# Attention with cached keys: another order of the keys, V loaded in longer runs, and the softmax denominator as two partial sums

## The chip, the cores and the metric

The kernel runs on one core of one Trainium2 chip. The metric is the time of one execution on the device in microseconds. A core has five engines with queues of their own: TensorE (PE in the profile, its weight loads PEld), VectorE (DVE), ScalarE (ACT), GpSimd (POOL) and SyncE (SP, which issues DMAs here). SBUF is the on-chip memory of 128 partitions, PSUM the memory that matmuls write into.

## The reference

Two blocks with an adaptive layer norm: attention with cached keys and values, then a mixer with an MLP. The change is in the first. Cut to it:

```python
def _A_ref(x, k_cache, v_cache, wq, wo):           # x: 2048 x 640, caches: 32 heads x 2048 keys x 128
    q = (x @ wq) ...                               # 32 heads x 2048 queries x 128
    scores = jnp.einsum('bhqd,bhkd->bhqk', q, k_cache) * Dh ** (-0.5)
    p = _softmax(scores, axis=-1)
    o = jnp.einsum('bhqk,bhkd->bhqd', p, v_cache)
    return (...o...).reshape(B, Sq, H * Dh) @ wo
...
h = _layernorm(x) * (1 + ca) + sa
x = x + ga * _A_ref(h, A_k_cache, A_v_cache, A_wq, A_wo)
h = _layernorm(x) * (1 + cb) + sb
x = x + gb * _B_ref(h, B_w1, B_w2, B_w3, B_w4)
```

All tensors are bf16. The softmax sums over all 2048 keys of a head, so the order in which the keys are taken does not matter as long as K and V follow the same order.

## The kernel before

**Stages.** A short start (layer norm, modulation, the first head's queries), the attention loop, the output projection with the second layer norm, and the mixer and MLP. The change lies in the loop and in what is set up for it.

**The loop.** 32 heads of 16 query tiles of 128 rows: 512 steps, and some more to drain. The program is written out by hand, step by step (line 516), as operations that each name what they read and write; a small planner (`Prog`, line 12) turns that into semaphore waits. Each engine runs its operations in the order in which they are written. A step s with tile j of head h has:

- `qk` (L286): 4 matmuls of 128x512 into Sps, two for each half of the 2048 keys.
- VectorE L559, once per half: reads the scores from PSUM, writes them negated and scaled into negS (three buffers) and accumulates the minimum per row. Its second row in the profile is DVE_READ_ACCUMULATOR.
- GpSimd L569: the smaller of the two minima, the bias of the exp.
- ScalarE L572: the exp over 2048 keys, into one of 8 slots of Pb.
- the transpose of that tile of probabilities, so that keys lie on partitions: by a DMA transpose from SyncE's queue (`transpose`, L222, one or two tiles at a time), for tiles 3 and 10 of each head by TensorE (`t_piece` L253, and copies L262 on ScalarE or L264 on VectorE). The target is one of 12 slots of PTs.
- `pv` (L299), 8 to 11 steps later: 16 matmuls of a tile, one for each 128 keys, with the transposed probabilities as weights and V as the moving operand. V lies in SBUF as `Vaug`, 16 groups of 130 columns: 128 of V, then two columns of ones. A matmul reads 129 of them, so column 128 of the result is the sum of the probabilities. Two tiles share a PSUM bank, 130 columns apart.
- ScalarE L550: copies two tiles' results from PSUM into Of.
- GpSimd, four steps after `pv`: for each four tiles `rcp` (L440, 128x4, the power -1 of the sums), then `norm` for each tile (L447, 128x128), and after the fourth a DMA that stores them to o_scratch in HBM (L454, issued on GpSimd).
- one fifth of the next head's query projection (`q_piece` L237, copied by `q_evac` L244) in most half steps.

**Loads of the next head.** All go out on SyncE's queue, in order with the transposes: K in tile 2 (`load_k`, L205, a DMA transpose from HBM, key k into column k), wq in tile 6 (L209), V in tile 12 (`load_v`, L214). K, V and wq have two buffers each. V's DMA takes key 128 t + p to partition p, group t: runs of 256 B.

**On GpSimd's queue.** In a step the L569 of that step comes first, then `rcp` and `norm`. An operation of GpSimd that reads what the operation before it wrote waits on a semaphore for it.

`small` is a small tensor for statistics of the first layer norm (columns 0 to 63, not needed in the loop, where columns 0 to 3 hold -1 for `rcp`) and for the minima and the reciprocals.

Of the kernel before, what the change touches and what calls it, by code (L numbers as in the profile page):

```python
# [7 lines left out]
BF16 = mybir.dt.bfloat16  # L8
F32 = mybir.dt.float32
# [106 lines left out]
def bass_adaLN_cond__mha_block_cached__mixer_s_mlp__prompt_kernel(  # L116
# [6 lines left out]
    KT = D // 128  # L123
    NQT = SQ // 128
    NQC = SQ // 512
    NKT = SK // 128
# [11 lines left out]
    with ExitStack() as es:  # L138
# [11 lines left out]
        if True:  # L150
            with ExitStack() as es1:
# [9 lines left out]
                kv = sb1("kv", [128, 2 * SK + 2 * NKT * 130 + 2 * KT * 128 + 2 * SQ], BF16)  # L161
                small = sb1("small", [128, 4 * NQT + 32], F32)
                hTx = sb1("hTx", [128, US], BF16)
# [4 lines left out]
                rstd = small[:, 3 * NQT:4 * NQT]  # L168
                nm0, nm1, nm, rl = [small[:, 4 * NQT + 8 * i:4 * NQT + 8 * i + 8] for i in range(4)]
                hT = hTx[:, 0:KT * SQ].rearrange("p (k q) -> p k q", k=KT)  # L170
# [3 lines left out]
                KTs = kv[:, 0:o1].rearrange("p (b s) -> p b s", b=2)  # L174
                Vaug = kv[:, o1:o2].rearrange("p (b k d) -> p b k d", b=2, k=NKT)
                wq = kv[:, o2:o3].rearrange("p (b k d) -> p b k d", b=2, k=KT)
# [26 lines left out]
                def load_k(h):  # L203
                    hb = h % 2
                    G.dma("sync", lambda e: e.dma_start_transpose(KTs[:, hb], A_k_cache[0, h]), ("k", hb), w=[("KT", hb)])  # L205

# [5 lines left out]
                def load_v(h):  # L212
                    hb = h % 2
                    G.dma("sync", lambda e: e.dma_start(Vaug[:, hb, :, 0:128], A_v_cache[0, h].rearrange("(t p) d -> p t d", p=128)),  # L214
                          ("v", hb), w=[("V", hb)])
# [76 lines left out]
                def pv(g, half):  # L292
                    hb = (g // NQT) % 2
                    b = g % RPT
                    ob = PO[:, ((g // 2) % 2) * 512 + (g % 2) * 130:]

                    def f(t):
                        for kt in range(half * 8, half * 8 + 8):
                            ins = t.matmul(ob[:, 0:129], PTs[:, b, kt, :], Vaug[:, hb, kt, 0:129],  # L299
                                           start=(kt == 0), stop=(kt == NKT - 1))  # L300
                        return ins
                    G.op("tensor", f, r=[("PT", b, half), ("V", hb), "ones"], w=[("O", (g // 2) % 2)])

# [28 lines left out]
                if H > 1:  # L332
# [8 lines left out]
                     r=["id0"], w=["ident"])  # L341
                G.op("gpsimd", lambda g: g.memset(Vaug[:, :, :, 128:130], 1.0), w=["ones"])
                G.op("scalar", lambda a: a.activation(s_col, c_sb, ACT.Silu), r=["c"], w=["scol"])
# [78 lines left out]
                mone = small[:, 0:4]  # L422
                G.op("gpsimd", lambda g: g.memset(mone, -1.0), w=["mone"] + [("mv", t) for t in range(NQT)])
                bank(("q", 0, NQC - 1))
# [13 lines left out]
                def rcp(gr):  # L438
                    b = gr % 2
                    G.op("gpsimd", lambda g: g.tensor_tensor(  # L440
                        out=rl[:, 4 * b:4 * b + 4], in0=Of[:].rearrange("p a z d -> p (a z) d")[:, 4 * b:4 * b + 4, 128],
                        in1=mone, op=ALU.pow),
                         r=[("Of", 2 * b), ("Of", 2 * b + 1), "mone"], w=[("rl", b)])

                def norm(gr, z):
                    b = gr % 2
                    G.op("gpsimd", lambda g: g.tensor_scalar(  # L447
                        out=On[:, b, z, :], in0=Of[:, 2 * b + z // 2, z % 2, 0:128],
                        scalar1=rl[:, 4 * b + z:4 * b + z + 1], scalar2=1.0, op0=ALU.mult, op1=ALU.mult),
                        r=[("Of", 2 * b + z // 2), ("rl", b)], w=[("On", b, z)])  # L450
# [65 lines left out]
                for s in range(at[-1] + LAG + 1):  # L516
                    h, j = divmod(s, NQT)
                    pvs = PVS.get(s, [])
                    evacs = []
                    if s <= 2:  # L520
                        for i in ((0,), (1, 2), range(3, len(MROW)))[s]:
                            mod_rows(i)
# [26 lines left out]
                    for p in [g_ // 2 for g_ in pvs if g_ % 2 == 1]:  # L549
                        G.op("scalar", lambda a, p=p: a.copy(  # L550
                            Of[:, p % 4].rearrange("p z d -> p (z d)")[:, 0:259], PO[:, (p % 2) * 512:(p % 2) * 512 + 259]),
                            r=[("O", p % 2)], w=[("Of", p % 4)])
# [291 lines left out]
```

## Time and profile before

| | |
|---|---|
| time, median of 3 runs | 1614.81 us (1610.35 to 1619.43) |
| the profiled execution, its time | 1604.1 us |
| its span, from first to last instruction | 1602.3 us |
| mean granted TensorE clock | 0.993 |
| busy share of the span: PE, DVE, ACT, POOL | 93%, 87%, 80%, 39% |
| DMA, mean over the span | 208 GB/s, 1,167,730 packets, 1,148,304 of them under 512 B |
| V load | 32 x 512 KB, 5.2 us from issue to landing (median) |
| K load, a transpose | 32, 4.6 us |
| transposes of probabilities | 256, 7.1 us |
| store of results to o_scratch | 128 x 128 KB, 4.5 us |

The profile is of one execution. Its groups name an operation as line, engine, operation, output<-input, shape and count, then its busy time in us and the mean of one in ns, then the idle time of the engine before it and what ended it. Overlapping rows of an engine count once in its busy time, and a single matmul's duration includes its latency, so the distance between starts is the better measure of its cost. The chain of waits follows back, from the last instruction of a window, what released each step. The issue of a DMA transpose on SyncE's queue has a duration that includes waiting for room.

### The profile page before, as it was taken

What the parts mean: (1) busy time and instruction counts of PE and PEld (TensorE: products, weight loads), DVE (VectorE), ACT (ScalarE), POOL (GpSimd) and SP (SyncE); (2) the same over time, 40 slices, a digit from 0 to 9 for tenths busy, and PEclk for the clock granted to TensorE, in tenths of its full rate; (3) what the DMA queues carried; (4) which work ended last, traced back from release to release, by engine and by line L of the source; (5) the groups of instructions that cost most, each with busy time, mean ns of one, the idle gap of its engine ahead of it and who ended that gap; (6) DMA issues with size and microseconds to landing.
All of it is one profiled execution on the core that took longest, in us unless ns stands there. A gap on an engine that the chain in (4) does not pass through costs nothing.

```text
span 1602.3 us, 34804 instructions
## 1 busy us (share of the span) xinstructions
PE 1492.6 (93%) x13978; PEld 963.0 (60%) x14231; DVE 1392.5 (87%) x2460; ACT 1288.2 (80%) x1145; POOL 622.8 (39%) x1394
## 2 busy tenths in 40 slices
PE   5799999999999999999999999999999799999998
PEld 3466666666666666666666666666666555545444
DVE  6999999999999999999999999999999266666424
ACT  4999999999999999999999999999999300055330
POOL 0144444444444444444444444444444423322000
PEclk9999999999999999999999999999999899999999
DMA  9999999999999999999999999999999994530000
GB/s 305 229 230 239 238 243 237 253 241 240 237 237 233 239 237 237 239 239 247 243 250 246 250 239 235 246 228 239 236 244 244 241 196 106 106 111 1 17 17 34
DMA packets 1167730, 333.62 MB, mean 208 GB/s; under 512 B 1148304, under 2 KB 1161552, under 8 KB 1167568
## 3 DMA queue, kind: packets, MB, share of 16 engines
q1 hardware_dynamic: 1161424, 314.59, 98.3%
q0 software_dynamic: 6144, 16.79, 3.3%
q8 instruction: 112, 1.84, 0.5%
q14 instruction: 50, 0.41, 0.1%
HBM read 43.48 MB, written 19.40 MB: 39 GB/s over the span
## 4 chain that ended last, share of the span: by engine, by line
DVE 30%; ACT 24%; PE 20%; DMA 15%; issue 10%; POOL 0%; SPq 0%; ACTq 0%; DVEq 0%
DVE negS L559 27%; ACT ring L572 19%; DMA ring<-ring 13%; PE Sps L631 8%; PE Sps L772 4%; PE Oaug L756 2%; PE QPp L756 2%; ACT ring L262 2%; ACT Of L550 2%; PE Sps L741 1%; ACT kv L244 1%; DMA ring<-in_A_x_dram 1%; DVE ring L364 1%; DMA negS<-o_scratch 1%; PE Sps L286 1%
## 5 line engine op out<-in xcount | busy, mean ns | idle before, releaser
L559 DVE TENSOR_SCALAR_CACHE_REDUCE negS<-Sps 128x1024 f32<-128x1024 f32 x1024 | 1177.2, 1220 | 22.2 <-PE Sps L286 12.5
L572 ACT ACTIVATE ring<-negS,small 128x2048 bf16<-128x2048 f32 x512 | 1011.4, 2029 | 21.9 <-DMA ring<-ring 15.7
L299 PEld LDWEIGHTS PTp<-kv,ring 128*128 128x128 bf16 x8192 | 560.0, 98 | 245.0 <-DMA ring<-ring 6.7
L286 PE MATMUL Sps<-kv 128*128 128x512 bf16 x1949 | 596.3, 383 | 62.8 <-DVE negS L559 42.9
L299 PE MATMUL PTp<-kv,ring 128*128 128x129 bf16 x8192 | 645.6, 221 | 6.5 <-DMA ring<-ring 5.6
L569 POOL TENSOR_SCALAR small<-small 128x1 f32<-128x1 f32 x512 | 145.8, 285 | 621.5 <-DVE negS L559 621.4
L286 PEld LDWEIGHTS Sps<-kv 128*128 128x128 bf16 x2048 | 124.5, 97 | 187.2 <-DVE negS L559 158.0
L447 POOL TENSOR_SCALAR On<-Of,small 128x128 bf16<-128x128 f32 x512 | 189.8, 371 | 13.0
L669 ACT COPY kv<-PTp 128x640 bf16<-128x640 bf16 x32 | 22.0, 692 | 155.0 <-PE PTp L666 154.9
L440 POOL TENSOR_TENSOR small<-Of,small 128x4 f32<-128x4 f32 x128 | 133.2, 1040 | 6.3 <-ACT Of L550 6.2
L454 POOL DMA_DIRECT2D o_scratch<-On x128 | 103.1, 806 | 40.8 <-POOL On L447 37.2
L237 PE MATMUL Oaug<-hTx,kv 128*128 128x512 bf16 x265 | 101.2, 387 | 7.9 <-ACT ring L262 4.2
L550 ACT COPY Of<-PTp 128x259 f32<-128x259 f32 x256 | 99.5, 389 | 10.5 <-PE PTp L299 10.5
L237 PE MATMUL QPp<-hTx,kv 128*128 128x512 bf16 x259 | 97.5, 381 | 2.5 <-ACT hTx L391 1.8
L559 DVE DVE_READ_ACCUMULATOR negS<-Sps 128x1 f32 x1024 | 85.4, 83 | 0.0
L612 POOL TENSOR_SCALAR On<-On 128x1 f32<-128x1 f32 x48 | 24.3, 507 | 152.9 <-DVE On L621 152.9
L639 DVE TENSOR_TENSOR ring<-Sps,mod_bc 128x640 f32<-128x640 f32 x16 | 13.2, 825 | 77.0 <-PE Sps L631 77.0
L631 PE MATMUL Sps<-wo,hTx 128*128 128x128 bf16 (+1 forms) x504 | 71.8, 304 | 5.0 <-DMA hTx<-o_scratch 4.7
L776 DVE TENSOR_TENSOR ring<-Sps,ring 128x640 f32<-128x640 f32 x16 | 13.2, 825 | 66.2 <-PE Sps L772 66.2
L631 PE MATMUL Sps<-wo,negS 128*128 128x128 bf16 (+1 forms) x504 | 69.1, 298 | 1.3 <-DMA negS<-o_scratch 0.9
L262 ACT COPY ring<-Oaug 128x1024 bf16<-128x1024 bf16 x64 | 66.2, 1034 | 0.0
L631 PEld LDWEIGHTS Sps<-wo,hTx 128*128 128x128 bf16 x512 | 40.2, 99 | 36.9 <-DMA hTx<-o_scratch 4.5
(82 smaller groups left out, 1011.2 us busy)
## 6 DMA issues: line engine op xcount, KB each, us to landing
kv<-in_A_v_cache_dram SPq DMA_DIRECT2D x32, 512.0 KB, 5.2
o_scratch<-On POOLq DMA_DIRECT2D x128, 128.0 KB, 4.5
ring<-in_A_x_dram SPq DMA_DIRECT2D x8, 640.0 KB, 4.9
kv<-in_A_wq_dram SPq DMA_DIRECT2D x32, 160.0 KB, 3.6
wo<-in_A_wo_dram SPq DMA_DIRECT2D x1, 5120.0 KB, 16.4
ring<-ring SPq DMA_TRANSPOSE x256, 7.1
ring<-in_w_mod_dram SPq DMA_DIRECT2D x1, 3200.0 KB, 13.6
out_dram<-wo SPq DMA_DIRECT2D x16, 160.0 KB, 1.8
```

The lines of the kernel that those rows point to most:

```text
L237: G.op("tensor", lambda t: t.matmul(JB[jb], wq[:, hb, q, :], hT[:, q, cc * 512:(cc + 1) * 512], start=(q == 0), stop=(q == KT - 1)), r=[(" ...
L262: G.op("scalar", lambda a: a.copy(dst, src), r=[("J", jb)], w=[("PT", g % RPT, r)])
L286: ins = t.matmul(Sps[:, col:col + 512], QT[:, hb, j * 128:(j + 1) * 128], KTs[:, hb, col:col + 512], start=True, stop=True)
L299: ins = t.matmul(ob[:, 0:129], PTs[:, b, kt, :], Vaug[:, hb, kt, 0:129], start=(kt == 0), stop=(kt == NKT - 1))
L440: G.op("gpsimd", lambda g: g.tensor_tensor(out=rl[:, 4 * b:4 * b + 4], in0=Of[:].rearrange("p a z d -> p (a z) d")[:, 4 * b:4 * b + 4, 128 ...
L447: G.op("gpsimd", lambda g: g.tensor_scalar(out=On[:, b, z, :], in0=Of[:, 2 * b + z // 2, z % 2, 0:128], scalar1=rl[:, 4 * b + z:4 * b + z ...
L454: G.dma("gpsimd", lambda e: e.dma_start(o_scr[jj // 2:jj // 2 + 2, :, hh].rearrange("a p z d -> p a (z d)"), On[:, b].rearrange("p (a z) d ...
L550: G.op("scalar", lambda a, p=p: a.copy(Of[:, p % 4].rearrange("p z d -> p (z d)")[:, 0:259], PO[:, (p % 2) * 512:(p % 2) * 512 + 259]), r= ...
L559: G.op("vector", lambda v, half=half, s=s, r8=r8: v.tensor_scalar(out=negS[:, s % 3, half * 1024:(half + 1) * 1024], in0=Sps[:, half * 102 ...
L569: G.op("gpsimd", lambda g, r8=r8: g.tensor_scalar(out=nm[:, r8:r8 + 1], in0=nm0[:, r8:r8 + 1], scalar1=nm1[:, r8:r8 + 1], scalar2=None, op ...
L572: G.op("scalar", lambda a, s=s, r8=r8: a.activation(Pb[:, s % RPB, :], negS[:, s % 3, :], ACT.Exp, bias=nm[:, r8:r8 + 1], scale=-1.0), r=[ ...
L631: ins = t.matmul(YB[b][:, c0:c0 + cw], OTj[pr % 2][:, 2 * hh + z, :], wo[:, hh, c0:c0 + cw], start=(hh == 0), stop=(hh == H - 1))
```

## The change

**Order of the keys.** Key 16 p + c now lies on partition p, in group c. K is loaded by a DMA transpose whose source is seen as 128 rows of 2048 elements (4096 B, 16 keys), in 16 blocks of 128 columns. The scores' columns, the probabilities and their transposes follow the same order.

**V.** A partition's 16 keys are consecutive in HBM (4096 B). The DMA writes them as 8 runs of two keys (512 B). In SBUF such a run lies between two columns of ones on either side (260 columns for two keys, the same room as before). The matmul of an even group reads the ones column ahead of its key and the key; that of an odd group reads the key and the ones column behind it. The first writes columns 0 to 128 of the result, the second columns 1 to 129: the values fall on columns 1 to 128 in both, the sum over even groups on column 0, that over odd groups on column 129.

**The first group.** The matmul that starts a tile has to set all 130 columns. So the first group reads from `V0`, which holds a one, the first key's values and a zero. Its two edge columns are set once; GpSimd copies the values from Vaug once a head, in tile 2, ahead of that step's L569. V0 lies in `small`, where the layer norm's statistics were.

**The sum.** ScalarE copies 260 columns of a pair of tiles instead of 259. GpSimd adds the two partial sums (128x4) and then takes the power -1.

```diff
-                small = sb1("small", [128, 4 * NQT + 32], F32)
+                small = sb1("small", [128, 4 + 130 + 2 + 32], F32)
...
+                V0 = small[:, 4:134].bitcast(BF16).rearrange("p (b d) -> p b d", b=2)
...
-                Vaug = kv[:, o1:o2].rearrange("p (b k d) -> p b k d", b=2, k=NKT)
+                Vaug = kv[:, o1:o2].rearrange("p (b k d) -> p b k d", b=2, k=NKT // 2)
...
-                    G.dma("sync", lambda e: e.dma_start_transpose(KTs[:, hb], A_k_cache[0, h]), ("k", hb), w=[("KT", hb)])
+                    G.dma("sync", lambda e: e.dma_start_transpose(
+                        KTs[:, hb].rearrange("p (c q) -> p c q", c=NKT), A_k_cache[0, h].rearrange("(q c) d -> q (c d)", c=NKT)), ("k", hb), w=[("KT", hb)])
...
-                    G.dma("sync", lambda e: e.dma_start(Vaug[:, hb, :, 0:128], A_v_cache[0, h].rearrange("(t p) d -> p t d", p=128)),
+                    G.dma("sync", lambda e: e.dma_start(Vaug[:, hb, :, 2:258], A_v_cache[0, h].rearrange("(p t z) d -> p t (z d)", t=NKT // 2, z=2)),
                           ("v", hb), w=[("V", hb)])
...
                         for kt in range(half * 8, half * 8 + 8):
-                            ins = t.matmul(ob[:, 0:129], PTs[:, b, kt, :], Vaug[:, hb, kt, 0:129],
+                            ins = t.matmul(ob[:, 0:130] if kt == 0 else ob[:, kt % 2:kt % 2 + 129], PTs[:, b, kt, :],
+                                           V0[:, hb] if kt == 0 else Vaug[:, hb, kt // 2, (1, 130)[kt % 2]:(130, 259)[kt % 2]],
                                            start=(kt == 0), stop=(kt == NKT - 1))
...
-                G.op("gpsimd", lambda g: g.memset(Vaug[:, :, :, 128:130], 1.0), w=["ones"])
+                for c0 in (0, 258):
+                    G.op("gpsimd", lambda g, c0=c0: g.memset(Vaug[:, :, :, c0:c0 + 2], 1.0), w=[("ones", c0)])
...
+                G.op("gpsimd", lambda g: g.memset(V0[:, :, 0:1], 1.0), w=["v0o"] + SMK)
+                G.op("gpsimd", lambda g: g.memset(V0[:, :, 129:130], 0.0), r=["v0o"], w=["v0e"])
...
                     G.op("gpsimd", lambda g: g.tensor_tensor(
-                        out=rl[:, 4 * b:4 * b + 4], in0=Of[:].rearrange("p a z d -> p (a z) d")[:, 4 * b:4 * b + 4, 128],
-                        in1=mone, op=ALU.pow),
+                        out=rl[:, 4 * b:4 * b + 4], in0=Og[:, :, 0], in1=Og[:, :, 129], op=ALU.add),
+                         r=[("Of", 2 * b), ("Of", 2 * b + 1)], w=[("rs", b), ("rl", b)])
+                    G.op("gpsimd", lambda g: g.tensor_tensor(
+                        out=rl[:, 4 * b:4 * b + 4], in0=rl[:, 4 * b:4 * b + 4], in1=mone, op=ALU.pow),
...
-                        out=On[:, b, z, :], in0=Of[:, 2 * b + z // 2, z % 2, 0:128],
+                        out=On[:, b, z, :], in0=Of[:, 2 * b + z // 2, z % 2, 1:129],
...
+                    if s < NG and j == 2:
+                        G.op("gpsimd", lambda g, hb=h % 2: g.tensor_scalar(
+                            out=V0[:, hb, 1:129], in0=Vaug[:, hb, 0, 2:130], scalar1=1.0, scalar2=1.0, op0=ALU.mult, op1=ALU.mult),
+                            r=[("V", h % 2), "v0e"], w=[("V0", h % 2)])
...
-                            Of[:, p % 4].rearrange("p z d -> p (z d)")[:, 0:259], PO[:, (p % 2) * 512:(p % 2) * 512 + 259]),
+                            Of[:, p % 4].rearrange("p z d -> p (z d)")[:, 0:260], PO[:, (p % 2) * 512:(p % 2) * 512 + 260]),
```

More of the change, by code (lines that the diff above doesn't have):

```diff
@@ L168, in bass_adaLN_cond__mha_block_cached__mixer_s_mlp__prompt_kernel @@
                 rstd = small[:, 3 * NQT:4 * NQT]
-                nm0, nm1, nm, rl = [small[:, 4 * NQT + 8 * i:4 * NQT + 8 * i + 8] for i in range(4)]
+                nm0, nm1, nm, rl = [small[:, 136 + 8 * i:136 + 8 * i + 8] for i in range(4)]
+                V0 = small[:, 4:134].bitcast(BF16).rearrange("p (b d) -> p b d", b=2)
                 hT = hTx[:, 0:KT * SQ].rearrange("p (k q) -> p k q", k=KT)
@@ L298, in f @@
                         for kt in range(half * 8, half * 8 + 8):
-                            ins = t.matmul(ob[:, 0:129], PTs[:, b, kt, :], Vaug[:, hb, kt, 0:129],
+                            ins = t.matmul(ob[:, 0:130] if kt == 0 else ob[:, kt % 2:kt % 2 + 129], PTs[:, b, kt, :],
+                                           V0[:, hb] if kt == 0 else Vaug[:, hb, kt // 2, (1, 130)[kt % 2]:(130, 259)[kt % 2]],
                                            start=(kt == 0), stop=(kt == NKT - 1))
                         return ins
-                    G.op("tensor", f, r=[("PT", b, half), ("V", hb), "ones"], w=[("O", (g // 2) % 2)])
+                    G.op("tensor", f, r=[("PT", b, half), ("V", hb), ("V0", hb), "v0e", ("ones", 0), ("ones", 258)], w=[("O", (g // 2) % 2)])
                 ringk = lambda a, b: [k for i in range(a // SK, -(-b // SK)) for k in (
@@ L422, in bass_adaLN_cond__mha_block_cached__mixer_s_mlp__prompt_kernel @@
                 mone = small[:, 0:4]
-                G.op("gpsimd", lambda g: g.memset(mone, -1.0), w=["mone"] + [("mv", t) for t in range(NQT)])
+                SMK = [("mv", t) for t in range(NQT)] + [("rstd", cc) for cc in range(NQC)]
+                G.op("gpsimd", lambda g: g.memset(mone, -1.0), w=["mone"] + SMK)
+                G.op("gpsimd", lambda g: g.memset(V0[:, :, 0:1], 1.0), w=["v0o"] + SMK)
+                G.op("gpsimd", lambda g: g.memset(V0[:, :, 129:130], 0.0), r=["v0o"], w=["v0e"])
                 bank(("q", 0, NQC - 1))
@@ L439, in rcp @@
                     b = gr % 2
+                    Og = Of[:].rearrange("p a z d -> p (a z) d")[:, 4 * b:4 * b + 4]
                     G.op("gpsimd", lambda g: g.tensor_tensor(
-                        out=rl[:, 4 * b:4 * b + 4], in0=Of[:].rearrange("p a z d -> p (a z) d")[:, 4 * b:4 * b + 4, 128],
-                        in1=mone, op=ALU.pow),
-                         r=[("Of", 2 * b), ("Of", 2 * b + 1), "mone"], w=[("rl", b)])
+                        out=rl[:, 4 * b:4 * b + 4], in0=Og[:, :, 0], in1=Og[:, :, 129], op=ALU.add),
+                         r=[("Of", 2 * b), ("Of", 2 * b + 1)], w=[("rs", b), ("rl", b)])
+                    G.op("gpsimd", lambda g: g.tensor_tensor(
+                        out=rl[:, 4 * b:4 * b + 4], in0=rl[:, 4 * b:4 * b + 4], in1=mone, op=ALU.pow),
+                         r=[("rs", b), "mone"], w=[("rl", b)])
                 def norm(gr, z):
```

## The prediction

> **What bounds the kernel now.** I read the stages first, then the chain of waits in two of them, then the queues. The attention loop runs 512 steps (32 heads of 16 tiles); its first and last L569 start at 38.0 and 1250.4 us, so 1212 of the 1602 us are this loop. The costliest groups in it:
>
> ```profile
> L559 DVE TENSOR_SCALAR_CACHE_REDUCE negS<-Sps 128x1024 f32<-128x1024 f32 x1024 | 1177.2, 1220 | 22.2 <-PE Sps L286 12.5
> L572 ACT ACTIVATE ring<-negS,small 128x2048 bf16<-128x2048 f32 x512 | 1011.4, 2029 | 21.9 <-DMA ring<-ring 15.7
> ```
>
> The chain of waits between 160 and 280 us is VectorE alone; two pieces one head apart:
>
> ```profile
> 185.35 5.37 DVE negS L559 x10
> 222.57 5.38 DVE negS L559 x10
> ```
>
> 222.57 - 185.35 = 37.22 us per head: VectorE's own pace, and the floor of the loop. Two stages by windows (columns: length, then busy us and instruction count of each engine):
>
> ```profile
> 160.00:340.00 180.00, 172.84 (x1773) 117.35 (x1803) 180.00 (x316) 180.00 (x151) 84.81 (x194) 1.00 1.20 242
> 380.00:740.00 360.00, 337.47 (x3436) 229.70 (x3498) 351.29 (x611) 350.52 (x292) 164.34 (x377) 1.00 1.23 238
> ```
>
> From 160 to 340 us VectorE (third pair) is busy throughout. From 380 to 740 us it runs 611 rows, at 65 rows a head 9.4 heads, 38.3 us each: 1.1 us over the floor. The waits say where that goes:
>
> ```profile
> ACT ring L572 <- DMA ring<-ring: 15.7, 26, 1.7
> DVE negS L559 <- ACT ring L572: 8.7, 15, 1.5
> ACT ring L572 <- POOL small L569: 5.8, 12, 1.0
> ```
>
> The exp (L572) needs a slot of Pb, which the DMA transpose of eight steps before has to release. 511 steps at the floor are 511 x 37.22 / 16 = 1189 us; the loop takes 1212, and some 4 of the 23 are the first head's start. So **about 19 us are stall**, 15.7 of it first seen as this wait. One head late in the loop, SyncE's queue and then ScalarE:
>
> ```profile
> 1061.26 0.58 SPq L214 DMA_DIRECT2D kv<-in_A_v_cache_dram  x1
> 1061.88 19.42 SPq L222 DMA_TRANSPOSE ring<-ring  x4
> ...
> 1099.99 0.58 SPq L214 DMA_DIRECT2D kv<-in_A_v_cache_dram  x1
> ```
>
> ```profile
> 1072.16 3.90 ACT L572 ACTIVATE ring<-negS,small 128x2048 bf16<-128x2048 f32 x2 [1.70 <-DMA ring<-ring]
> ...
> 1081.92 3.90 ACT L572 ACTIVATE ring<-negS,small 128x2048 bf16<-128x2048 f32 x2 [0.64 <-DMA ring<-ring]
> ```
>
> The V load goes out at 1061.26, the transposes behind it land late, and the exp waits 10.9 and 20.7 us after it. Of the 26 waits, 10 lie about 10 us after a V load (7.5 us together) and 7 about 20 us after one (3.7 us, the same backlog handed on).
>
> **The change part by part.**
>
> *V in runs of 512 B.* The same 512 KB per head, 1024 packets instead of 2048. DMA rate in 40 slices from 192.1 to 194.1 us, where transposes give way to a V load:
>
> ```profile
> GB/s 141 317 256 317 266 307 276 302 302 276 302 271 307 266 317 266 307 271 297 225 230 205 241 230 230 205 220 241 220 225 236 220 200 241 236 225 230 205 220 236
> ```
>
> The last 21 slices average 225 GB/s, so V takes 524 KB / 225 = 2.33 us of all 16 engines, 18.2 ns per 256 B packet and engine. The trace has no 512 B packet. Nearest rows: x in packets of 1280 B (11 to 14 us):
>
> ```profile
> DMA packets 897, 1.18 MB, mean 393 GB/s; under 512 B 30, under 2 KB 843, under 8 KB 897
> ```
>
> which is 1280 x 16 / 393 = 52.1 ns a packet. Between 18.2 and 52.1, a packet of 512 B takes a quarter of the way: 26.7 ns, and 64 per engine 1.71 us: **0.62 us saved per head**. Bounds: nothing, if the bytes set the price, and 1.16 us, if the packets do. The Trainium skill ("DMA: Bandwidth & Descriptors", Specifications) gives 512 B as the least transfer for line rate; by it V would run at the 393 GB/s of the x rows, 1.33 us, and save 1.0.
>
> What lies behind V gains: the transposes in the same queue. Cutting each of the 10 waits by up to 0.62 gives 5.0 us, each of the 7 behind them 3.1: **8 us**. The other nine waits (4.5 us) stay.
>
> *K from rows of 4096 B.* The same packets of 256 B through the transpose. The first K, from contiguous keys, runs at 291 GB/s (16.3 to 17.3 us); transposes of o_scratch, also out of HBM but across rows of 16 KB, at 290 (1266 to 1268.5); those from SBUF at 290. I take 0. Issue on SyncE: 2.11 us median for K now, 1.63 at least for a one-tile transpose of the new form, so at best 0.5 us per head; I leave it out, since that duration includes waiting. The skill speaks against it (same page, Latency and other measured facts): a transpose with a non-contiguous middle dimension gets 261 GB/s, a contiguous one 350 to 400. By that K would lose some 0.6 us a head and eat V's gain; the three rows above show no such difference.
>
> *GpSimd.* Now, around one reciprocal:
>
> ```profile
> 207.28 0.28 POOL L569 TENSOR_SCALAR small<-small 128x1 f32<-128x1 f32 x1 [0.58 <-DVE negS L559]
> 207.54 1.04 POOL L440 TENSOR_TENSOR small<-Of,small 128x4 f32<-128x4 f32 x1
> 208.69 0.37 POOL L447 TENSOR_SCALAR On<-Of,small 128x128 bf16<-128x128 f32 x1
> ```
>
> Added: 128 adds of 128x4 and 32 copies of 128x128. The copy is the shape of L447, 0.37 us; it stands ahead of the L569 of a head's third step, where GpSimd otherwise idles 1.65 us, and its V was issued six steps (14 us) earlier and lands in 5.2. No cost; without that idle time 32 x 0.37 = 12 us. The add has no row. pow takes 0.55 us for one element (L614, median) and 1.04 for four, 0.16 per element on a base of 0.39; single-input operations cost 0.285 (1 element) to 0.37 (128), so elements of an add are almost free: 0.39 us, bounds 0.28 and 1.04, plus 0.1 for the wait between it and pow (the gap now seen between pow and norm). After the norm GpSimd idles 0.5 us before the next L569, so 0.49 just fits. Behind a late L569 stands the exp, and behind that the transposes. At the tail of the loop the last add is bare: +0.5 us.
>
> *PV matmuls.* 7 of 16 per tile now read V from an odd column, 2 bytes past a 4-byte boundary, and write PSUM one column further; one is 130 wide. PE has little room:
>
> ```profile
> 605.06 0.63 PE L299 MATMUL PTp<-kv,ring 128*128 128x129 bf16 x8
> 605.53 0.38 PE L237 MATMUL Oaug<-hTx,kv 128*128 128x512 bf16 x1
> 605.75 0.59 PE L286 MATMUL Sps<-kv 128*128 128x512 bf16 x2
> ```
>
> Half a step starts at 604.63 and the next at 605.75: 1.12 us of matmuls against 37.22 / 32 = 1.163 per half step. Eight PV matmuls in 0.63 us, 0.22 of it the last one's latency, are 58.6 ns apart. No row has an odd start. V's rows of 260 B already start at 4-byte, not 8-byte, boundaries without cost, so I take 0. Bounds: 0, since nothing gets shorter, and another 58.6 ns for each odd start.
>
> ScalarE copies 260 columns instead of 259: 0.39 us either way. The memsets and the first V0 copy lie ahead of the loop.
>
> *Sum.* Profiled span 1602.3 - 8 + 0.5 = 1594.8; the execution around it 1604.1 - 7.5 = 1596.6. The runs' median, 1614.8, is 10.7 us above that execution. I take the difference for more of the same stalls (19 + 11 = 30 us) and scale: 8 x 30 / 19 = 12.4, so 1614.8 - 12.4 + 0.5 = **1603 us**.
>
> **The rivals.**
>
> *V's load was not what was late.* Of the stall, 4.5 us of waits lie elsewhere, and another wait (instruction fetches stop the transposes too: no bytes for over 1 us near 190 us) may keep the backlog; or the run is split into 256 B packets after all; or K loses what V gains. Then about 1613 us (1607 to 1621). For it: heads at the floor carry the same V load.
>
> *The whole backlog goes.* The waits feed each other (exp late, transpose late, exp late eight steps on), so 0.6 to 1.0 us a head may be enough to stay at the floor. Some 2 of the 30 us are waits that no DMA starts (PE for ScalarE's L262): 1614.8 - 28 + 0.5 = 1587. For it: heads 1 to 9 all hold 37.22.
>
> *Odd starts cost TensorE.* From 43 ns / 3.5, some 12 ns for each odd matmul, PE becomes the bound. At a doubled pace half a step takes 1.12 + 3.5 x 0.0586 = 1.325, +0.162 over 1.163, in the 28 of 32 half steps of a head that carry a fifth piece: 28 x 32 x 0.162 = 145 us, 1760 us. Against it: the unaligned rows already there. The skill ("SBUF — State Buffer", Operand start alignment) allows such starts for other engines and says that nothing was timed.
>
> *The add delays the exp.* From 0.4 us on, the add is more than GpSimd's idle time. At 1.04 us the next L569 comes 0.65 us late, 128 times; ScalarE starts an exp up to 1.1 us after its L569 ends, which covers about half. 128 x 0.3 = 38 us: 1650 us. For it: pow costs 1.04.
>
> **How the numbers follow.** Forecast 0.45 (own range 1598, with V's saving at 1.16 us, which cuts the 17 waits by 10.6 us, to 1607, with nothing scaled), no relief 0.22, all relief 0.15, odd starts 0.09, late exp 0.09. The runs before spread over 0.56%, so 0.5% (8 us) is what can be told from no change. Faster, under 1606.7: 0.33 of the forecast's 0.45 and the 0.15 of all relief, 0.48. Same: 0.12 and 0.19, 0.31. Slower: 0.03 + 0.09 + 0.09 = 0.21. A range from 1586 to 1621 holds the forecast, the no-relief case and most of all relief, 0.8; the two dear cases lie outside.
>
> **What would show it.** Right: 1024 packets a head fewer, V's stretch near 310 GB/s, the waits of L572 for the DMA halved, more heads at 37.22 us. PV matmuls further apart than 59 ns would show the odd starts; L572 waiting for GpSimd's L569 far more than 5.8 us, the add. Waits for the DMA unchanged at a shorter V would show that V was not the cause.

## The result, and the profile after

The changed kernel takes 1629.58 us (median of 5 runs, 1627.69 to 1630.01); the kernel before, measured beside it, 1610.35 us (median of 5, 1603.12 to 1619.43). The ratio is 1.0108, 95% interval 1.0082 to 1.0135: slower by some 17 us, where 1603 us had been forecast. The profiled execution of the changed kernel took 1630.01 us with a span of 1628.2, against 1602.3 before. The pace from one head's first step to the next's shows where: before, heads 1 to 9 ran at VectorE's 37.2 us and the later ones at 37.2 to 40.5; after, only heads 1 to 5 hold 37.2, and the rest take 37.6 to 40.3.

The costliest groups on the page of the changed kernel (busy us and mean ns, then idle us ahead of them and what ended most of it):

```profile
L573 DVE TENSOR_SCALAR_CACHE_REDUCE negS<-Sps 128x1024 f32<-128x1024 f32 x1024 | 1181.3, 1224 | 41.1 <-PE Sps L288 20.4
L586 ACT ACTIVATE ring<-negS,small 128x2048 bf16<-128x2048 f32 x512 | 1007.2, 2015 | 41.9 <-POOL small L583 24.8
```

L573 is the old L559, L586 the old L572, L583 the old L569. VectorE's work is the same, but its idle time in the loop has grown from 22.2 to 41.1 us, and the exp now waits longest for GpSimd. The waits of the changed kernel (total us, times, longest):

```profile
POOL small L531 <- DMA kv<-in_A_v_cache_dram: 100.2, 29, 5.7
ACT ring L586 <- POOL small L583: 24.8, 37, 2.0
...
DVE negS L573 <- ACT ring L586: 19.4, 43, 2.0
ACT ring L586 <- DMA ring<-ring: 16.8, 35, 1.5
```

The first line is new: GpSimd's copy of V's first group (L531) waits for V in 29 of 32 heads, 3.5 us each. Behind it in GpSimd's queue stands L583, whose result is the exp's bias; that wait went from 5.8 us to 24.8. The wait of the exp for the DMA, which the longer runs of V were to halve, did not fall (15.7 before, 16.8 now). One such place, GpSimd's queue first, then ScalarE's:

```profile
1087.81 0.30 POOL L531 TENSOR_SCALAR small<-kv 128x128 bf16<-128x128 bf16 x1 [4.21 <-DMA kv<-in_A_v_cache_dram]
1088.09 0.27 POOL L583 TENSOR_SCALAR small<-small 128x1 f32<-128x1 f32 x1
```

```profile
1088.40 3.90 ACT L586 ACTIVATE ring<-negS,small 128x2048 bf16<-128x2048 f32 x2 [1.24 <-POOL small L583]
...
1093.73 3.90 ACT L586 ACTIVATE ring<-negS,small 128x2048 bf16<-128x2048 f32 x2 [0.69 <-DMA ring<-ring]
```

V of this head was issued at 1082.56 and landed at 1087.8. The copy stood waiting for 4.21 us, the exp got its bias 1.24 us late, and VectorE followed (its next half step at 1090.52 waited 0.77 us for TensorE).

The two kernels side by side, over each V load, show the second half of the story. The DMA rate in 40 slices of 0.15 us, from the issue of a V load on; the kernel before from 647.54 us, then the changed kernel from 654.82, and last one microsecond of the latter (1.5 to 2.5 us after the issue):

```profile
GB/s 295 292 285 294 290 288 294 283 295 240 232 213 193 225 273 266 256 265 266 256 256 236 239 227 247 220 220 68 77 212 294 288 292 287 292 294 287 288 285 282
DMA packets 6019, 1.53 MB, mean 255 GB/s; under 512 B 6019, under 2 KB 6019, under 8 KB 6019
```

```profile
GB/s 297 283 294 290 290 290 292 285 171 101 58 17 38 41 41 102 82 174 201 212 304 290 317 348 355 324 328 311 295 167 150 128 251 294 282 297 292 283 299 280
DMA packets 4387, 1.37 MB, mean 229 GB/s; under 512 B 3363, under 2 KB 4387, under 8 KB 4387
```

```profile
DMA packets 100, 0.05 MB, mean 51 GB/s; under 512 B 0, under 2 KB 100, under 8 KB 100
```

Both begin with transposes at 290 GB/s that were queued ahead of V. Before, V follows without a break and runs at 190 to 275 GB/s until the 27th slice. After, the rate first falls to 17 to 102 GB/s for more than a microsecond (slices 10 to 17), and only then do the longer packets flow, at 290 to 355. The text calls this the hole. It does not lie ahead of V's packets: none of the 100 packets of the last line is under 512 B, so they are all V's own, and they come slowly. By packet sizes, which tell V apart only in the new form, V's 1024 packets spread over 3.1 us from first to last (median of 28 loads), although one takes 27 ns, as forecast. From issue to landing a V load takes as long as before; both pages have this line:

```profile
kv<-in_A_v_cache_dram SPq DMA_DIRECT2D x32, 512.0 KB, 5.2
```

Single loads differ; the means over 28 loads come with the experiments.

### The profile page after: what moved, and what is told of

Its sections match the earlier page's. It is cut to its first block, busy times and chain, and to the rows that moved or that the text cites. A ratio compares the mean times of both kernels' runs of the same rounds, so it can differ in the third digit from the quotient of the medians.

```text
span 1628.2 us, 34967 instructions
## 1 busy us (share of the span) xinstructions
PE 1490.7 (92%) x13978; PEld 962.6 (59%) x14231; DVE 1396.7 (86%) x2460; ACT 1291.2 (79%) x1145; POOL 656.9 (40%) x1557
## 4 chain that ended last, share of the span: by engine, by line
ACT 29%; DMA 21%; PE 20%; DVE 17%; issue 8%; POOL 3%; SPq 1%; ACTq 0%; DVEq 0%; POOLq 0%
ACT ring L586 23%; DVE negS L573 15%; DMA ring<-ring 13%; PE Sps L645 7%; DMA kv<-in_A_v_cache_dram 6%; PE Sps L786 4%; ACT ring L264 3%; ACT Of L564 2%; PE Oaug L770 2%; PE QPp L770 2%; PE Sps L755 1%; SPq L224 1%; ACT kv L246 1%; DMA ring<-in_A_x_dram 1%; POOL o_scratch L464 1%
## 5 line engine op out<-in xcount | busy, mean ns | idle before, releaser
L573 DVE TENSOR_SCALAR_CACHE_REDUCE negS<-Sps 128x1024 f32<-128x1024 f32 x1024 | 1181.3, 1224 | 41.1 <-PE Sps L288 20.4
L586 ACT ACTIVATE ring<-negS,small 128x2048 bf16<-128x2048 f32 x512 | 1007.2, 2015 | 41.9 <-POOL small L583 24.8
L301 PE MATMUL PTp<-kv,ring 128*128 128x129 bf16 x7680 | 614.9, 221 | 0.0
L301 PEld LDWEIGHTS PTp<-kv,ring 128*128 128x128 bf16 x7680 | 508.8, 98 | 177.1
L583 POOL TENSOR_SCALAR small<-small 128x1 f32<-128x1 f32 x512 | 146.1, 285 | 498.8 <-DVE negS L573 497.4
L451 POOL TENSOR_TENSOR small<-small 128x4 f32<-128x4 f32 x128 | 133.1, 1040 | 10.0
L464 POOL DMA_DIRECT2D o_scratch<-On x128 | 103.3, 807 | 41.1 <-POOL On L457 37.5
L301 PE MATMUL PTp<-small,ring 128*128 128x130 bf16 x512 | 112.8, 220 | 7.3 <-DMA ring<-ring 7.3
L564 ACT COPY Of<-PTp 128x260 f32<-128x260 f32 x256 | 96.5, 377 | 11.3 <-PE PTp L301 11.2
L301 PEld LDWEIGHTS PTp<-small,ring 128*128 128x128 bf16 x512 | 50.1, 98 | 68.1 <-DMA ring<-ring 8.4
L573 DVE DVE_READ_ACCUMULATOR negS<-Sps 128x1 f32 x1024 | 89.1, 87 | 0.0
```

What stands on the lines that cost most here:

```text
L301: ins = t.matmul(ob[:, 0:130] if kt == 0 else ob[:, kt % 2:kt % 2 + 129], PTs[:, b, kt, :], V0[:, hb] if kt == 0 else Vaug[:, hb, kt // 2, ...
L451: G.op("gpsimd", lambda g: g.tensor_tensor(out=rl[:, 4 * b:4 * b + 4], in0=rl[:, 4 * b:4 * b + 4], in1=mone, op=ALU.pow), r=[("rs", b), "m ...
L464: G.dma("gpsimd", lambda e: e.dma_start(o_scr[jj // 2:jj // 2 + 2, :, hh].rearrange("a p z d -> p a (z d)"), On[:, b].rearrange("p (a z) d ...
L564: G.op("scalar", lambda a, p=p: a.copy(Of[:, p % 4].rearrange("p z d -> p (z d)")[:, 0:260], PO[:, (p % 2) * 512:(p % 2) * 512 + 260]), r= ...
L573: G.op("vector", lambda v, half=half, s=s, r8=r8: v.tensor_scalar(out=negS[:, s % 3, half * 1024:(half + 1) * 1024], in0=Sps[:, half * 102 ...
L583: G.op("gpsimd", lambda g, r8=r8: g.tensor_scalar(out=nm[:, r8:r8 + 1], in0=nm0[:, r8:r8 + 1], scalar1=nm1[:, r8:r8 + 1], scalar2=None, op ...
```

## The experiments

Two theories stood at the start. W: the copy's wait for V is the loss. Q: the new order of K and V in HBM costs DMA time (the expectations call this T, the transfers). Later a third question came in: is V's load what stalls the kernel at all, and what is a shorter one worth? Each ratio is to runs of the kernel before on the same chip; the groups of runs were on different chips.

**Copy later.** `late_copy` is the changed kernel with one number changed:

```
-                    if s < NG and j == 2:
+                    if s < NG and j == 6:
```

> The changed kernel with one thing moved: GpSimd copies V0 in tile 6 of a head instead of tile 2, some 9 us later and still two steps ahead of the first matmul that reads it. Theory W (the wait): GpSimd's copy waits for the V load, 100 us in 29 waits, and holds back the L583 behind it and so the exp; with the copy late enough the waits for V and the exp's 24.8 us of waiting for GpSimd go, and the time falls back to the kernel before or below it by V's shorter load: 1598 to 1612 us. Rival T (the transfers): the new order of K and V makes the transposes late by itself; then the exp's waits for the DMA stay at some 17 us in 35 waits and the time stays above 1620 us.

Measured: 1632.32 us, ratio 1.0063 (1.0040 to 1.0086). Its waits:

```profile
ACT ring L586 <- DMA ring<-ring: 42.3, 52, 3.2
...
ACT ring L586 <- POOL small L583: 6.3, 11, 1.0
```

The copy no longer waits, and the exp waits for GpSimd as little as before (6.3 us). But the time comes back as waits for the DMA, 42.3 us. Against the changed kernel's 1.0108 some 0.45% is won (the two intervals make that 0.1 to 0.8%); 0.6% is left that is not the copy's wait.

**The copy alone.** `before_copy` is the kernel before with a copy of V's first group in the third step of each head; nothing reads it.

```
+                    if s < NG and j == 2:
+                        G.op("gpsimd", lambda g, hb=h % 2: g.tensor_scalar(
+                            out=V0[:, hb, 1:129], in0=Vaug[:, hb, 0, 0:128], scalar1=1.0, scalar2=1.0, op0=ALU.mult, op1=ALU.mult),
+                            r=[("V", h % 2), "v0e"], w=[("V0", h % 2)])
```

> The kernel before, with nothing of the change but a copy of V's first group (128x128) on GpSimd in tile 2 of each head, at the same place in its queue, whose result nobody reads. K, V and the sums are as before. Theory W: the wait alone costs what the change cost, 15 to 25 us above the kernel before, with about 100 us of GpSimd waiting for V. Rival T: the copy is 32 x 0.3 us on an engine that is 40% busy, no change beyond 5 us.

Measured: 1625.25 us, ratio 1.0018 (1.0002 to 1.0034).

```profile
POOL small L524 <- DMA kv<-in_A_v_cache_dram: 94.6, 28, 5.5
ACT ring L579 <- POOL small L576: 22.8, 32, 2.5
...
ACT ring L579 <- DMA ring<-ring: 13.6, 18, 1.7
```

The same waits as in the changed kernel, yet only 0.2%: where the exp is held by GpSimd it is held less by the DMA. W is real but small: 3 us where its expectation had 15 to 25.

**The key order alone.** `key_order` is the kernel before with both loads in the order 16 p + c, V still in 256 B runs:

```
-  e.dma_start_transpose(KTs[:, hb], A_k_cache[0, h])
+  e.dma_start_transpose(KTs[:, hb].rearrange("p (c q) -> p c q", c=NKT), A_k_cache[0, h].rearrange("(q c) d -> q (c d)", c=NKT))
-  A_v_cache[0, h].rearrange("(t p) d -> p t d", p=128)
+  A_v_cache[0, h].rearrange("(p t) d -> p t d", t=NKT)
```

> The kernel before with the new order of the keys alone: K through the transpose from rows of 4096 B, V's partition from 16 consecutive keys but still in 16 runs of 256 B between the old columns; no V0, no second sum. Theory W: K's transpose moves as fast as before (4.7 us to landing against 4.6), no change, within 0.4% of the kernel before. Rival T: if K's new rows are what makes the transposes late, 1620 us and more.

Measured: 1634.07 us, ratio 1.0073 (1.0049 to 1.0098), the exp waiting 36.6 us for the DMA. A second time, on another chip (`key_order_2`):

> The kernel before with the new key order alone (K from rows of 4096 B, V in 16 consecutive keys per partition, still 256 B runs), a second time, on a chip of its own. If the 0.7% of the first time belongs to the order: 1.005 to 1.010 again. If it was that chip's: 1.000 to 1.004, the sum of the two halves measured apart (0.06% and 0.17%).

Measured: 1631.26 us, ratio 1.0064 (1.0035 to 1.0092), 32.2 us of waits for the DMA. So Q holds for the order as a whole. Its halves, each alone:

> The kernel before with K loaded through the transpose from rows of 4096 B, V unchanged; keys and values then no longer match, so the attention's result is another. The order of the keys in both K and V together cost 0.73% (1634 against 1623 us). Theory K: the transpose that steps over 4096 B rows of HBM is what costs, +0.5 to 1.0% here and none in the run with V's rows alone. Rival V: nothing here, within 0.3%.

> The kernel before with V loaded so that a partition takes 16 consecutive keys, still in 256 B runs, K unchanged; keys and values no longer match. Theory K: nothing, within 0.3% of the kernel before. Rival V: the engines then read HBM 4096 B apart at the same time, and the whole 0.7% is here, with V's landing later than 5.2 us.

Measured: K's rows alone (`k_rows`) 1619.11 us, ratio 1.0006 (0.9990 to 1.0023); V's 16 consecutive keys alone (`v_rows`) 1620.12 us, ratio 1.0017 (0.9997 to 1.0036). They add up to 0.23%, the whole is 0.6 to 0.7%. That the two together cost more than the halves is measured; why is open. The unchanged kernels on that chip:

> The kernel before, unchanged, for a profile on the same chip as the others. Both theories: the time of the kernel before. If the stalls are what makes it slower on this chip than in the profile at hand, its exp waits for the DMA well above 15.7 us.

> The changed kernel, unchanged, beside the parts of it on one chip. If the parts add up, the order of the keys (0.7%) and GpSimd's wait for V (0.2 to 0.45%) make the 1.1%: ratio 1.008 to 1.013. If the wait counts for nothing beside the order of the keys, it comes out at 1.006 to 1.008, like the kernel with the late copy.

Measured: 1614.01 us, ratio 0.9991 (0.9970 to 1.0011), and 1634.05 us, ratio 1.0102 (1.0080 to 1.0123). The profile of `before_again` has 23.5 us in 33 waits of the exp for the DMA, where the one of before has 15.7 in 26: this sum moves by half between executions of one kernel, and only larger differences of it mean something.

**Is V what stalls the kernel?** `no_v_load` and `half_v` are the kernel before with less of V:

```
-                        if j == PVD + 1 and h + 1 < H:
+                        if j == PVD + 1 and h + 1 < 2:
```

```
-  Vaug[:, hb, :, 0:128], A_v_cache[0, h].rearrange(...)
+  Vaug[:, hb, 0:NKT if h < 2 else NKT // 2, 0:128], A_v_cache[0, h, 0:SK if h < 2 else SK // 2].rearrange(...)
```

> The kernel before with V loaded for heads 0 and 1 alone; from the third head on the old values stay, so the output differs, and 30 loads of 512 KB are gone. It gives the upper bound of what a shorter V can bring. As the prediction had it (the waits behind a V load are V's), all 17 such waits go: 11 us less wait of the exp for the DMA and, scaled as in the prediction, 12 to 28 us less time, ratio 0.983 to 0.992. Rival (the load only decides which transpose is late, the backlog has other causes): waits of the exp for the DMA stay at 10 us or more, ratio 0.995 to 1.0.

> The kernel before with half of V loaded from the third head on (1024 of 2048 packets of 256 B; the other half of the keys keep old values). V's stretch falls by 1.1 us a head, which is 1.8 times what the prediction gave V's new runs. If the gain goes with V's time: half of the 2.2% that the whole load is worth, ratio 0.987 to 0.991. If it takes most of V's time to be gone before anything is won: 0.995 to 1.0. If a small relief is enough, as the rival of the whole backlog had it: 0.978 to 0.983.

Measured: without V 1586.09 us, ratio 0.9783 (0.9749 to 0.9817); with half of V 1589.86 us, ratio 0.9842 (0.9817 to 0.9866). What is left of VectorE's and the exp's longer waits in the loop of `half_v`:

```profile
DVE negS L559 <- PE Sps L286: 6.2, 3, 2.2
ACT ring L572 <- POOL small L569: 5.2, 13, 1.0
```

The exp never waits for the DMA any more, and all heads from 1 to 31 stand at 37.0 to 37.4 us, with half of V as with none. So V's load was the right thing to shorten: 25.5 us (1.58% of 1616.7) for 30 heads with 1.17 us less V each (half of the prediction's 2.33), 0.73 us of time for every microsecond. As the floor is reached, this is a least value: less than half of V may already be enough. The two loops are equally long (1195.5 and 1195.3 us); the ratios differ because the kernel before took 1616.66 us on the one chip and 1620.89 on the other, and because the medians lie 3.8 us apart where the profiled executions do not (1586.12 us with half of V, 1586.35 without).

**Which part of V's new form takes that back?** Five kernels take the change and its parts apart. `late_old_k` and `after_old_k` are `late_copy` and the changed kernel with K loaded as before:

> The changed kernel with the copy of V0 in the seventh step of a head and with K in its old key order (keys and values then do not match): what is left of the change is V in 512 B runs, the add and the copy, without the copy's wait. If K's new rows are what costs the 0.6% that the late copy still showed: ratio 0.998 to 1.001, and the exp waits for the DMA 15 to 25 us instead of 42. If V's new runs are the cost, or the add and the copy: 1.004 to 1.008 again.

> The changed kernel with K in its old key order alone (keys and values then do not match). If the wait of the copy for V is the whole loss: ratio 1.008 to 1.012 as for the changed kernel. If K's rows add their part to it: 1.003 to 1.006, with some 28 waits of the copy for V and about 25 us of the exp for GpSimd either way.

Measured: 1628.76 us, ratio 1.0055 (1.0032 to 1.0078), and 1634.60 us, ratio 1.0084 (1.0057 to 1.0112). K's rows are not the main cost in the changed kernel: with its old rows the loss stays.

`v512_only` leaves out the copy and the add too; `no_copy` leaves out the copy alone; `add_only` puts nothing but the add into the kernel before. The core of the edits:

```
# no_copy and v512_only: the first matmul of a tile
-  V0[:, hb] if kt == 0 else Vaug[...]
+  Vaug[:, hb, 0, 1:131] if kt == 0 else Vaug[...]
# v512_only: rcp
+  in0=Of[:].rearrange("p a z d -> p (a z) d")[:, 4 * b:4 * b + 4, 129], in1=mone, op=ALU.pow
# add_only: rcp
+  in0=Og[:, :, 128], in1=zero, op=ALU.add
```

> The changed kernel without the copy and the add and with K's old rows: what is left is V in 512 B runs between two columns of ones, read from odd columns too (the first group takes an element of V into its 130th column, one of the two partial sums is used, and keys and values do not match). If the 512 B runs bring what the prediction said and GpSimd takes it back: 0.988 to 0.996. If the runs themselves bring nothing: 0.998 to 1.002. If they cost: 1.003 to 1.007.

> The kernel before with one more add of 128x4 on GpSimd ahead of each of the 128 pows (it adds zeros, the result is the same). By the prediction's step: no cost, 0.998 to 1.002. If the add is what takes V's gain back: 1.003 to 1.007, with the exp's wait for GpSimd's minimum well over 6 us in 12.

> The changed kernel without the copy of V0: the first PV matmul of a tile reads V itself in 130 columns (so one of the two partial sums has an element of V in it). New K rows, V in 512 B runs, odd starts and the add stay. If the copy's wait is the greater part of the loss: 0.998 to 1.003. If it was only a part, as the late copy showed: 1.004 to 1.007.

Measured: `v512_only` 1621.23 us, 1.0034 (1.0015 to 1.0053); `add_only` 1617.54 us, 1.0016 (0.9995 to 1.0038), the exp waiting for GpSimd 6.5 us in 12, as before; `no_copy` 1628.14 us, 1.0076 (1.0046 to 1.0106). V's new load, without copy, add and K's rows, costs 0.3% where it was to gain 0.8%. A V load of `v512_only`, from its issue at 652.84 us:

```profile
GB/s 237 292 282 297 287 290 294 288 287 112 24 27 55 38 154 106 137 38 20 113 157 225 331 352 355 338 352 348 297 289 283 217 63 201 292 290 288 288 292 294
```

The same hole at V's start as in the changed kernel, without K's rows, copy or add. Two things had changed about V's runs: their length, and that the runs of a partition lie next to each other in HBM (4096 B). `pairs_only` keeps the length and undoes the other:

```
-  A_v_cache[0, h].rearrange("(p t z) d -> p t (z d)", t=NKT // 2, z=2)
+  A_v_cache[0, h].rearrange("(t p z) d -> p t (z d)", p=128, z=2)
```

> As v512_only (no copy, no add, K's old rows; keys and values do not match, one partial sum has an element of V in it), but V's 512 B runs are taken from keys 256 t + 2 p and 256 t + 2 p + 1, so that a partition's runs lie 64 KB apart instead of adjacent. If the hole ahead of V's packets belongs to the 4096 B order in HBM: the rate 2 us after V's issue stays near 170 GB/s instead of 42, and 0.65 us less V a head is won: ratio 0.986 to 0.994. If the hole belongs to the 512 B packets: it stays below 100 GB/s, ratio 0.999 to 1.005.

Measured: 1618.72 us, ratio 0.9964 (0.9939 to 0.9989). A V load of it, from 651.10 us:

```profile
GB/s 10 72 283 295 287 292 292 287 290 290 296 246 195 164 137 157 82 184 222 236 314 341 338 338 331 300 283 217 128 87 186 292 288 292 290 287 292 292 288 292
```

Here the hole is shallower and the packets flow just as fast, at 300 to 341 GB/s. In the mean over 28 loads it is deep all the same: in the lowest quarter of a microsecond between 1.5 and 2.5 us after the issue the rate is 76 GB/s, against 42 in `v512_only`, 78 in `v_rows` and 138 to 175 with V loaded as before. What differs is how long it lasts: V's first 100 packets take 0.4 to 0.45 us (medians) in the three kernels with this order, and 0.8 to 1.1 us in the seven with 512 B runs and 16 consecutive keys, over loads that meet no fetch of instructions; the whole of V takes 2.9 to 3.0 us against 3.0 to 3.2. So the rate of 170 did not come, while its ratio nearly did. Against `v512_only` the order of the runs is worth 0.7% (0.4 to 1.0%).

**A kernel from it that computes everything.** `pairs` adds the late copy and the add, leaves K's load as it was, and reads K's columns at a stride of two, so that keys match:

```
+  Sps[:, col:col + 512].rearrange("p (t z q) -> p t z q", z=2, q=128), QT[...],
+  KTs[:, hb, col:col + 512].rearrange("p (t q z) -> p t z q", z=2, q=128)
```

> The same V order in a kernel that computes everything: K's old load, the score matmuls read K's columns at a stride of two, the copy of V0 in a head's seventh step, the add. If the order in HBM was the cause and stride two costs TensorE nothing: 0.987 to 0.997. If the 512 B packets are the cause: 1.002 to 1.007 as for late_old_k. If stride two slows the score matmuls: over 1.02, with the L286 pairs longer than 0.59 us.

> The same kernel as pairs, a second time on a chip of its own, in five rounds. If the 512 B packets in this order are worth what pairs_only showed (0.4%) and the late copy and the add take half of it: 0.996 to 0.9995. If they take all of it: 0.9995 to 1.003.

Measured: 1619.91 us, ratio 0.9982 (0.9958 to 1.0005), and the second time 1612.88 us against 1615.88, ratio 0.9979 (0.9961 to 0.9997). It is faster than the kernel before by 0.2%, about as little as can be seen. Stride two costs TensorE little (391 ns a matmul in the mean, 383 before).

**The hole, counted.** From the packets of each trace I summed, over the 5.5 us that begin 0.5 us after each V issue, how much fewer bytes came than at 290 GB/s, as a time: once over the 8 to 20 loads of a kernel that meet no fetch of instructions (standard errors 0.03 to 0.10 us), once over all 28 after 160 us (0.06 to 0.15); and the first of these over K's loads as well (16 to 20 loads, 0.03 to 0.12). A fetch is a packet of 8 or 16 KB on one of the profile's two instruction queues: in the kernel before, the rest of the traffic falls from some 265 to about 105 GB/s for 1.25 us around one, in the mean.

| kernel | V, no fetch, us | V, all loads, us | K, no fetch, us | ratio |
|---|---|---|---|---|
| before, before_again, add_only, before_copy | 0.74, 0.89, 0.85, 0.89 | 1.36, 1.48, 1.57, 1.44 | 0.66, 0.72, 0.63, 0.81 | 1, 0.9991, 1.0016, 1.0018 |
| half_v (fewer bytes to move) | 0.63 | 1.17 | 0.59 | 0.9842 |
| k_rows, v_rows | 0.88, 0.99 | 1.36, 1.36 | 0.82, 0.71 | 1.0006, 1.0017 |
| key_order, key_order_2 | 1.08, 1.11 | 1.55, 1.51 | 0.87, 0.93 | 1.0073, 1.0064 |
| v512_only, no_copy | 1.21, 1.22 | 1.34, 1.46 | 0.63, 0.77 | 1.0034, 1.0076 |
| after, after_again | 1.18, 1.16 | 1.32, 1.46 | 0.74, 0.85 | 1.0108, 1.0102 |
| late_copy, late_old_k, after_old_k | 1.35, 1.30, 1.43 | 1.49, 1.50, 1.50 | 0.91, 0.74, 0.78 | 1.0063, 1.0055, 1.0084 |
| pairs_only, pairs, pairs_2 | 1.10, 1.10, 1.12 | 1.34, 1.32, 1.27 | 0.80, 0.69, 0.66 | 0.9964, 0.9982, 0.9979 |

Where no fetch falls into the load, V's new form costs the transposes 0.3 to 0.6 us more than before. Such a load lands 5.0 to 5.2 us after its issue (medians of the ten profiles with 512 B runs), against 4.7 to 4.8 in the four of the first row. More of the old form's loads meet a fetch (18 to 20 of 28, against 8 to 15), and over all loads the two forms cost nearly the same (1.27 to 1.50 us against 1.36 to 1.57). By neither count does the new form save the 0.62 us of the forecast. That much is shown.

How far does this go towards the times? At the 0.73 us of time per microsecond of `half_v`, what the two columns without a fetch add to the means of the first row makes, as an estimate, 0.2% for `k_rows` and for `v_rows`, 0.6 and 0.7% for the key order, 0.4% for `v512_only` and 0.6% for `no_copy`. All of these lie in the measured intervals, as do `late_old_k` and `after_old_k` (0.7 and 0.9%); `late_copy` (1.0%) lies above its own, and the changed kernel (0.5 and 0.6%) below, where the copy's wait comes on top. For the three kernels whose runs lie 64 KB apart the same estimate gives a loss of 0.3 to 0.5%, where 0.2 to 0.4% was gained. So the count fits the loss with 16 consecutive keys and does not explain the gain of the other order; the path of that 0.7% is open.

## Why the prediction was wrong

**What bounds the kernel: right.** The stall of the loop is the DMA queue's, V's load is in it, and relief there would have paid: the prediction priced 32 x 0.62 us of V at 12.4 us, 0.62 us of time per microsecond; `half_v` gives at least 0.73. The rival "the whole backlog goes" had the right idea of how steep this is: half of V, 1.17 us a head, brings every head to the floor; its 0.6 to 1.0 us were not tried. Of the signs that the prediction named, the 1024 packets fewer and a stretch near 310 GB/s came, the halved waits and the further heads at 37.22 us did not. The unchanged waits do not clear V, since its load did not become shorter.

**The step that failed first: "64 per engine 1.71 us: 0.62 us saved per head".** The price of a packet was right, 27 ns against the 26.7 forecast. But a load's length is not its packets times their price: the packets spread over 3.1 us, because for about a microsecond the first of them come slowly, and by landing and by the count above the load became no shorter (5.2 us for all loads, 5.0 to 5.2 against 4.7 to 4.8 without a fetch). The bounds, from nothing to 1.16 us saved, left out that it could become longer. The forecast had no term for the start of a load; it read the price from the stretch in which V already flowed. Nor had it one for where the runs lie in HBM, though that is half of the edit: the same 512 B runs are worth 0.9964 or 1.0034 by that alone. The rule of 512 B for full line rate from the Trainium skill ("DMA: Bandwidth & Descriptors", Specifications) fits the flowing part (290 to 355 GB/s against 190 to 275 before, though below the 393 of the x rows), and by it alone the saving would have been larger still; the traces show that the slow start uses the gain up.

**The second: "No cost" for the V0 copy.** The working said that its V "was issued six steps (14 us) earlier and lands in 5.2". The six steps were counted in the order of the program. SyncE's queue runs behind it, since its transposes wait there for ScalarE. The trace of before had it: V of one head goes out at 1061.26 us, and the L569 ahead of which the copy was to stand comes here:

```profile
1063.73 0.28 POOL L569 TENSOR_SCALAR small<-small 128x1 f32<-128x1 f32 x1 [1.67 <-DVE negS L559]
```

2.5 us, not 14; in 25 of the 31 later heads the distance is below 5.2. The price was bounded at 12 us "without that idle time"; as a wait of 100 us on an in-order queue it costs 0.2% alone (`before_copy`, 3 us) and perhaps 0.3 to 0.45% in the changed kernel (against `no_copy`, whose interval overlaps, and `late_copy`).

**K's rows at 0: right within the error alone, not together with V's.** The time is 1.0006 alone. The transfers are not quite free: by the count, K's loads cost 0.84 us in the mean of the seven profiles with the new rows and 0.71 in the eleven with the old ones and a full V, so 0.13 us more a head, some 3 us by the price above (an estimate); the landing is 4.6 us before, 4.7 in the changed kernel and 5.0 in `k_rows`. Together with V's 16 consecutive keys the order cost 0.6 to 0.7%, twice, more than the halves' times add up to; whether the two act on each other is open. The Trainium skill's lower rate for such a transpose ("DMA: Bandwidth & Descriptors", Latency and other measured facts) would have been 0.6 us a head by the prediction's estimate, some 0.9% at 0.73; the run of K's rows alone, at most 0.23%, does not show it.

**The add: right, and cheaper than thought.** 0.196 us in the mean, forecast 0.39. Alone it stays at 1.0016, not told apart from nothing, and the exp waits for GpSimd no more than before.

**Odd starts: right.** The PV matmuls keep their 221 ns and their pace; that rival is gone.

**How the loss adds up.** `pairs_only` -0.36%; 16 consecutive keys to a partition +0.7% (`v512_only` +0.34%); add and K's rows +0.4% (`no_copy` +0.76%; alone 0.16 and 0.06%); the copy's wait +0.3% (the changed kernel, +1.08% and +1.02%). The first two differ clearly; the last two steps have intervals of about 0.4% each, and the order of the terms matters.

**Range and chances.** The slower side held two cases, odd starts and a dear add, and neither came. The case without relief named K's loss and a split of the packets, not a V load that starts more slowly. A wait of the copy for V should have been a case too: it needed only the distance between two rows of the trace.

## What to carry to other kernels

Whether an operation finds its input ready is read from times in the trace, on the queue that issues the load, and never from steps of the program: here SyncE's queue, which runs in order and waits, left 2.5 us of the 14. The length of a DMA is its start, its packets and its end; when its form changes, the price of a flowing packet says nothing about the start, so try the new access pattern alone before building work around it. And where one load is known to set the stall, fewer bytes (half of V: 1.6%) are worth far more than longer packets (0.4% at best here).

## What the runs showed of the hardware

V's load in 512 B packets from HBM behind DMA transposes starts slowly here: without a fetch, the rate (in slices of 0.1 us) lies below 100 GB/s for 0.8 to 1.2 us of the 5.5 us counted, in all ten profiles with such packets, and for 0.15 to 0.4 us with 256 B packets as before. Addresses count as well: 256 B runs of 16 consecutive keys per partition have 0.4 to 0.6 us. The Trainium skill ("DMA: Bandwidth & Descriptors", Latency and other measured facts) gives an HBM access as 0.2 us in the mean and 2 us at high load, which would allow for such a hole; no run here shows that this is its cause.

Relief of the DMA queue is worth the same from some point on: half of V gone brings every head to 37.2 us, and the other half adds nothing to the pace of the loop (1195.5 and 1195.3 us from its first to its last L559).
